# Reciprocals spread over a head's rows by DMA in fp32 instead of by products on TensorE, in a kernel of memory-augmented attention and a spectral filter

## The chip, the cores and the metric

The kernel runs on one core of a Trainium2 chip. A core has TensorE (PE, with its weight loads shown as PEld), VectorE (DVE), ScalarE (ACT), GpSimd (POOL), and SyncE (SP), which here issues nearly all DMAs. The metric is the device time of one execution in microseconds; three executions of the kernel before took 710.68, 711.77 and 715.36 us, median 711.77.

## The reference

Two independent parts share the program and are set side by side in the output. Part A is attention with a memory, 2048 tokens of 576 features, 32 heads of 18, in 4 segments of 512 tokens:

```python
for s in range(N):                                   # 4 segments
    p = _softmax(einsum("bhqd,bhkd->bhqk", qs, ks) * scale + mask)
    a_dot = einsum("bhqk,bhkd->bhqd", p, vs)
    num = einsum("bhld,bhde->bhle", phi(qs), M)
    den = einsum("bhld,bhd->bhl", phi(qs), z)[..., None] + 1e-6
    o = g * num / den + (1.0 - g) * a_dot
    M = M + einsum("bhld,bhle->bhde", phi(ks), vs)
    z = z + einsum("bhld->bhd", phi(ks))
return o.transpose(...).reshape(B, S, D) @ wo
```

M and z are zero in the first segment, so the memory counts from the second on. Part B is a two-dimensional real FFT of [2048, 576], a product with complex weights and the inverse; the change does not touch it.

## The kernel before, in words

The first half of the program (to about 356 us) does the FFT, the projections to q, k and v, and the memories M (`Mst`) and z (`zst`) of segments 1 to 3. What the change touches is the second half, `attention`, a loop over `t` from 0 to 132. **One `t` is one head step**: four segments of 32 heads make 128 steps. A step holds, for head `t+11`, the scores for the row maxima (`s1`: scores into PSUM, DVE maxima `mx` and `junk`), and for head `t` the scores again with the maximum folded in and the three exponentials on ACT (`s2`, L703, L708, L712). Every fourth step POOL zeroes the upper triangle of four heads (L716), and over the next four steps PE multiplies these heads by the values (`pv`, L731, sixteen matmuls in two batches of eight). The maxima of four heads go through POOL (`mh`, L682 and L683), a transpose on PE (L686), ACT, and a DMA that ACT issues (L692) into the row of the queries that carries them.

The unnormalised output `U` of eight heads goes to DRAM, its rows as `uD` and the softmax sums as `rD`. The normalisation follows a segment later. With 18 rows a head, the 576 rows of a segment are cut into five tiles of 126, 126, 126, 126 and 72 rows (7 heads and 4 heads), by 512 tokens; the order is `ORD = (4,0,1,2,3)`. For a segment the work is:

- `den`: z times phi(q) on PE (`pd`) to `dD`.
- `recip`, once for the softmax sums (times 1-g) and once for `den` (times g): load, add epsilon, reciprocal on DVE, gate on ACT. Before, ACT and POOL then split the result into three bf16 parts (L760 to L763), a DMA writes them to DRAM (L765), and another loads them as 96 rows of 512 (`rr`, `rd`, L769).
- `combine`: for each tile a matmul with the 0/1 table `sel` spreads the reciprocals of 7 heads over 126 rows in PSUM (`pb`, L851), DVE multiplies the tile `ux` of `uD` by it (L854 or L856), POOL adds the memory part `am` (L857, from the second combination on), ACT rounds (`oh`, L836), POOL takes the rest (`ol`, L841).
- `mem1`: for each tile a product of M with phi(q) on PE (`pn`, L804), a copy out of PSUM by ACT (L806; DVE at the end), another `pb` (L810) and a product on DVE (L811).
- `oproj`: the output projection, 16 pieces of seven matmuls for a segment (`po`, L874).

The last segment's normalisation and projection stand behind the loop (`last_tile`, `last_proj`).

The order is written by hand. Each engine runs its instructions in program order, so a wait stops all that stands behind it on that engine. Two mechanisms place the work beside the head steps: a **lane** gives one piece per step to each generator in it; the **background queue** `bg` is a list, taken in order, from which `run_bg(1.2)` takes 1.2 pieces a step. Before, `recip` is in the lane and `combine` and `mem1`, interleaved by `mixed`, in the background queue, and then `oproj`. `later(1, f)` puts an issue of a DMA at the end of the next step. All of these DMAs are in SP's queue with the loads of stacked queries and keys (`Qs`, `Ks`, L635 and L637), which are needed 3 and 8 steps later.

PSUM has one bank, `post`, for `pn`, `pb`, `pd` and `po`, and three each for the two kinds of scores. In SBUF `ux` has three buffers.

Of the kernel before, what the change touches and what calls it, by code (L numbers as in the profile page):

```python
# [363 lines left out]
def atables():  # L364
    sel=np.zeros((96,5,126),np.float32)
    for t in range(5):
        for p in range(126 if t<4 else 72):
            h=7*t+p//18
            sel[h::32,t,p]=1
# [5 lines left out]
    return dict(sel=sel.reshape(96,-1),bm=bm.reshape(126,-1),mask=mask,ident=np.eye(128,dtype=np.float32),neg1=-np.ones((2,4096),np.float32))  # L375
# [9 lines left out]
class ATT:  # L385
# [189 lines left out]
    def att_setup(s,cp):  # L575
# [10 lines left out]
        s.rrD=[d(f"rrD{i}",[96,512],BF) for i in range(4)]  # L586
        s.rdD=[None]+[d(f"rdD{i}",[96,512],BF) for i in range(1,4)]
# [20 lines left out]
    def late_setup(s,cp):  # L608

        nc,io=s.nc,s.io; q=[]  # L610
        s.sel=cp.tile([96,5,126],BF,name="sel",bufs=1); nc.gpsimd.dma_start(s.sel,io["sel"].rearrange("p (t m) -> p t m",t=5))
# [137 lines left out]
    def recip(s,src,dst,gate,eps,load,slack=0):  # L749
        nc=s.nc; tp=s.tp  # L750
        w=tp.tile([128,3,128],BF,name="rw",bufs=2); y=tp.tile([128,128],F32,name="ry",bufs=2)
# [12 lines left out]
        for _ in range(slack): yield  # L764
        nc.sync.dma_start(bass.AP(tensor=dst.tensor,offset=dst.offset,ap=[[128,128],[32*512,3],[1,128]]),w)  # L765
        yield
        yield
        r=tp.tile([96,512],BF,name=load,bufs=1)
        nc.sync.dma_start(r,dst)  # L769
        s.rc[load]=r  # L770
        yield
# [6 lines left out]
    def den(s,g,lane):  # L778
# [12 lines left out]
        def chain():  # L791
            yield
            yield
            yield
            yield from s.recip(s.dD[g],s.rdD[g],s.gt,True,"rd",2)
# [5 lines left out]
    def mem1(s,g,t):  # L801
# [4 lines left out]
        (nc.vector.tensor_copy if s.now>=119 else nc.scalar.copy)(am[:r],pn[:r])  # L806
        if g<3: s.later(1,lambda: s.pq_load(g+1,t))
        yield
# [17 lines left out]
    def combine(s,g):  # L826
# [4 lines left out]
        yield  # L831
        yield
        def high(u):
            r=126 if u<4 else 72
            s.oh[u]=tp.tile([128,512],F32R,name="oh",bufs=5); s.ol[u]=tp.tile([128,512],F32R,name="ol",bufs=5)
            (nc.vector.tensor_copy if s.now>=119 else nc.scalar.copy)(s.oh[u][:r],s.am[u][:r])  # L836
        def low(u):
            r=126 if u<4 else 72
            A,B=s.oh[u],s.ol[u]
            l=B if u<4 else tp.tile([128,512],F32R,name="ol4",bufs=1)  # L840
# [5 lines left out]
        for t in range(7+late):  # L846
            if t>1 and not late: high(ORD[t-2]); low(ORD[t-2])
            if t<5:
                i=t; t=ORD[t]; r=126 if t<4 else 72; x=xs[t]
                pb=s.post("pb")  # L850
                nc.tensor.matmul(pb[:r],s.sel[:,t,:r],s.rc["rr"],start=True,stop=True)  # L851
# [27 lines left out]
    def last_tile(s,t,rc):  # L879

        nc=s.nc; r=126 if t<4 else 72; x=s.ux[t]
        pb=s.ps.tile([128,512],F32,name="pb",tag="post")
        nc.tensor.matmul(pb[:r],s.sel[:,t,:r],s.rc[rc],start=True,stop=True)
        nc.vector.tensor_tensor(x[:r],x[:r],pb[:r],op=OP.mult)
# [27 lines left out]
    def begin(s,sm,sp,ps1):  # L912
# [3 lines left out]
        s.mg={};s.mx={};s.m2={};s.P={};s.vs={};s.rc={};s.am={};s.pq={};s.ux={};s.potag=None  # L916
# [18 lines left out]
    def homes(s):  # L935

        for n,t,b in (("oh",F32R,5),("ol",F32R,5),("am",F32,5),("pq",F32,5),("ux",F32,3),("ol4",F32R,1)): s.tp.tile([128 if n in ("oh","ol","ux","ol4") else 126,512],t,name=n,bufs=b)
# [215 lines left out]
```

## Time and profile before

| | |
|---|---|
| three executions, us | 710.68, 711.77, 715.36 |
| profiled execution, us | 710.93 |
| its span, us | 709.2 |
| PE, PEld busy | 679.2 us (96%), 501.4 us (71%) |
| DVE, ACT, POOL busy | 551.2 us (78%), 451.3 us (64%), 209.8 us (30%) |
| moved by DMA | 123.80 MB, mean 175 GB/s |
| head steps | from 356.6 us to about 668 us |

The durations are those of the profiled execution. In rows of groups the first number behind the bar is the busy time in us, the second the mean in ns of one instruction, and then comes the engine's idle time ahead of them. In rows of stretches the columns are the stretch and its length, then for PE, PEld, DVE, ACT and POOL the busy time and the count of instructions, the granted clock, the mean busy share of the sixteen DMA engines, and GB/s. Matmuls are pipelined: the durations of neighbours overlap, and what one costs is seen from the start of the next.

### The profile page before, as it was taken

Reading aid. Unit: us, or ns where it says so; the run is one execution under the profiler, and the core shown is the slowest. Engines: PE = TensorE matmul, PEld = TensorE weight load, DVE = VectorE, ACT = ScalarE, POOL = GpSimd, SP = SyncE. Lnnn points to the kernel's source line nnn. Section 1 sums busy time; section 2 is a strip of 40 time slices with the busy share of each in tenths; the row PEclk is TensorE's granted clock in tenths of the full one; section 3 lists DMA queues with packets and bytes.
Section 4 is the critical chain, followed back from the end, with each engine's and each line's share of the span. In section 5 each row is a group of like instructions: output and inputs, shape, how many; then the busy total and the mean of one; then the engine's idle time right before and its main releaser. Section 6 shows DMA issues by size and latency. Waiting matters only on the chain. (4 is left out here: it accounts for less than half of the span.)

```text
span 709.2 us, 14404 instructions
## 1 busy us (share of the span) xinstructions
PE 679.2 (96%) x4991; PEld 501.4 (71%) x4991; DVE 551.2 (78%) x1262; ACT 451.3 (64%) x986; POOL 209.8 (30%) x403
## 2 busy tenths in 40 slices
PE   4999999999999999999999899999999999999997
PEld 4988869879879879999954454445566445663487
DVE  5999979899799779787787887888657876567533
ACT  3665797485587474544378777777656776567421
POOL 5432000100200102655235333444323652235300
PEclk9999999999999999999999999999999999999999
DMA  8996455576385688899339886886656767442152
GB/s 308 289 286 171 132 159 185 162 208 203 91 234 177 167 209 294 199 253 262 110 111 207 182 175 137 197 202 159 152 131 176 190 159 158 89 127 67 28 156 82
DMA packets 71146, 123.80 MB, mean 175 GB/s; under 512 B 12184, under 2 KB 39174, under 8 KB 67482
## 3 DMA queue, kind: packets, MB, share of 16 engines
q1 hardware_dynamic: 64422, 106.89, 57.3%
q0 software_dynamic: 5632, 15.76, 8.2%
q8 instruction: 39, 0.64, 0.4%
q10 hardware_dynamic: 1020, 0.25, 0.2%
q14 instruction: 33, 0.27, 0.2%
HBM read 82.10 MB, written 39.81 MB: 172 GB/s over the span
## 5 line engine op out<-in xcount | busy, mean ns | idle before, releaser
L661 DVE CUSTOM_DVE_ANT_0 junk<-s,x 128x512 bf16<-128x512 f32 x248 | 137.0, 552 | 57.9 <-PE s L653 53.1
L716 POOL TENSOR_SCALAR_AFFINE_SELECT P<-P 128x512 f32<-128x512 f32 (+2 forms) x132 | 78.4, 625 | 113.6 <-ACT P L703 104.8
L667 DVE TENSOR_REDUCE mx<-s 128x4 f32<-128x512 f32 x128 | 87.7, 685 | 5.2 <-PE s L666 3.3
L703 ACT ACTIVATE P<-s 128x512 f32<-128x512 f32 x128 | 77.7, 607 | 12.6 <-PE s L702 4.6
L731 PE MATMUL pv<-P,vs 128*32 128x512 f32 (+3 forms) x1024 | 82.5, 439 | 0.1
L708 ACT ACTIVATE P<-s 128x512 f32<-128x512 f32 x128 | 77.5, 606 | 2.4 <-PE s L707 2.2
L712 ACT ACTIVATE P<-s 128x256 f32<-128x256 f32 x128 | 49.9, 390 | 44.7 <-PE s L711 44.2
L653 PE MATMUL s<-Ks,Qs 108*128 108x384 bf16 (+3 forms) x256 | 69.1, 301 | 1.5 <-DVE mx L667 1.2
L731 PEld LDWEIGHTS pv<-P,vs 128*32 128x32 f32 x1024 | 26.9, 109 | 45.3 <-issue 34.5
L461 PE MATMUL pj<-x,wqkh 128*128 128x512 f32 x162 | 56.5, 409 | 0.0
L653 PEld LDWEIGHTS <-Qs 108*128 108x128 bf16 x320 | 31.5, 98 | 24.4 <-issue 13.0
L205 DVE TENSOR_TENSOR Z<-t,t 128x290 f32<-128x290 f32 (+1 forms) x96 | 48.4, 555 | 0.1
L519 POOL MEMSET vt<- 128x32 f32 x16 | 2.4, 167 | 149.0 <-PE pm L529 127.7
L205 DVE TENSOR_TENSOR t<-Z 128x580 f32<-128x580 f32 x64 | 46.1, 757 | 0.0
L142 PE MATMUL f<-ftab,eh 128*128 128x290 f32 (+1 forms) x160 | 32.6, 323 | 11.8 <-DMA ftab<-ftab 9.2
L666 PE MATMUL s<-tri,idb 128*128 128x128 bf16 x256 | 43.0, 219 | 0.0
L295 PE MATMUL i<-civ,Y 128*128 128x256 f32 (+1 forms) x288 | 39.3, 289 | 0.2 <-POOL Y L280 0.2
L295 PEld LDWEIGHTS i<-civ,Y 128*128 128x128 f32 (+1 forms) x288 | 36.6, 181 | 1.0 <-POOL Y L280 0.4
L306 PE MATMUL i<-itab,T 128*128 128x290 f32 (+1 forms) x224 | 36.7, 306 | 0.0
L142 PEld LDWEIGHTS f<-ftab,eh 128*128 128x128 f32 (+1 forms) x160 | 26.1, 206 | 14.0 <-issue 8.6
L461 PE MATMUL pj<-x,wqkl 128*128 128x512 f32 x90 | 35.5, 395 | 0.0
L461 PE MATMUL pj<-xh,wqkl 128*128 128x512 f32 x90 | 35.5, 395 | 0.0
(210 smaller groups left out, 1830.2 us busy)
## 6 DMA issues: line engine op xcount, KB each, us to landing
qkD<-sp SPq DMA_DIRECT2D x32, 384.0 KB
xin<-xb SPq DMA_DIRECT2D x16, 384.0 KB
cfw<-cfw POOLq DMA_DIRECT2D x16, 384.0 KB, 4.3
civ<-civ POOLq DMA_DIRECT2D x16, 384.0 KB, 8.8
vs<-vD SPq DMA_DIRECT2D x16, 330.0 KB
vD<-vt SPq DMA_DIRECT2D x16, 311.0 KB
W<-w SPq DMA_DIRECT2D x16, 290.0 KB
yb<-yout SPq DMA_DIRECT2D x16, 290.0 KB
```

The lines of the kernel that those rows point to most:

```text
L142: nc.tensor.matmul(p[:,r,:FP],x,t,start=n==0,stop=n==6)
L205: v.tensor_tensor(o,a,b,op=op)
L295: nc.tensor.matmul(p[:m,k],Y[i][:,q,c*128:c*128+m],cc[:,hl,o:o+256],start=n==0,stop=n==5)
L461: s.nc.tensor.matmul(out,a,b,start=i==0,stop=i==len(L)-1)
L653: nc.tensor.matmul(out,Q[:108,h,128*i:128*i+128],K[:108,h,:128*(i+1)],start=True,stop=True)
L661: nc.vector.tensor_tensor_reduce(out=junk[:,:w],in0=src,in1=s.mask[:,512-w:],scale=1.0,scalar=-3.0e38, op0=OP.add,op1=OP.max,accum_out=s.m ...
L667: nc.vector.tensor_reduce(out=s.mx[k][:,hh],in_=pa.rearrange("p (b c) -> p b c",c=128),axis=mybir.AxisListType.X,op=OP.max)
L703: nc.scalar.activation(P[0][:,hh],p0,AF.Exp,scale=SC)
L708: nc.scalar.activation(P[1][:,hh],p1,AF.Exp,scale=SC)
L712: nc.scalar.activation(P[2][:,hh],p2,AF.Exp,scale=SC)
L716: nc.gpsimd.affine_select(out=x[:,r],in_=x[:,r],pattern=[[0,r.stop-r.start],[1,128]],compare_op=OP.is_ge,fill=0.0,base=0,channel_multiplie ...
L731: nc.tensor.matmul(s.pvt[32*hh:32*hh+32,128*j:],vt[:,j,19*h:19*h+32],mv[0][:,hh,mv[1]],start=j==0,stop=j>1,skip_group_check=True)
```

## The change

The reciprocals are no longer split into bf16 parts. `recip` writes 64 KB of fp32, and for each tile `bt_load` reads them back with a row repeated 18 times, so that a tile `bt` of 126 rows by 512 in SBUF holds the factors. It has three buffers, and the next load is put in SP's queue one step after a tile was used. There are 35 of these loads: 20 for the four combinations and 15 for the memory. The 35 `pb` matmuls, the table `sel`, the loads `rr` and `rd`, the ACT and POOL work of the split, and the copy out of PSUM in `mem1` go: DVE multiplies `pn` from PSUM by `bt` at once. `combine` moves from the background queue into the lane, one tile per head step; the five `mem1` become background pieces of one step each, and the background rate goes from 1.2 to 0.8. A buffer for `ol` is saved.

```diff
-    def recip(s,src,dst,gate,eps,load,slack=0):
+    def recip(s,src,dst,gate,eps):
...
         nc.scalar.activation(y,y,AF.Copy,scale=gate)
-        nc.scalar.copy(w[:,0],y)
-        nc.gpsimd.tensor_tensor(y,y,w[:,0],op=OP.subtract)
-        nc.gpsimd.tensor_copy(w[:,1],y)
-        nc.gpsimd.tensor_tensor(w[:,2],y,w[:,1],op=OP.subtract)
...
-        r=tp.tile([96,512],BF,name=load,bufs=1)
-        nc.sync.dma_start(r,dst)
...
+        nc.sync.dma_start(dst.rearrange("h (b c) -> (h b) c",b=4),y)
+    def bt_load(s):
+        if not s.bsrc: return
+        a,t=s.bsrc.pop(0); w=7 if t<4 else 4
+        x=s.tp.tile([126,512],F32,name="bt",bufs=3)
+        a=a[7*t]
+        s.nc.sync.dma_start(x[:18*w],bass.AP(tensor=a.tensor,offset=a.offset,ap=[[512,w],[0,18],[1,512]]))
+        s.bts.append(x)
...
-        (nc.vector.tensor_copy if s.now>=119 else nc.scalar.copy)(am[:r],pn[:r])
+        nc.vector.tensor_tensor(am[:r],pn[:r],s.bts.pop(0)[:r],op=OP.mult)
+        s.later(1,s.bt_load)
...
-        pb=s.post("pb")
-        nc.tensor.matmul(pb[:r],s.sel[:,t,:r],s.rc["rd"],start=True,stop=True)
-        nc.vector.tensor_tensor(am[:r],am[:r],pb[:r],op=OP.mult)
...
-    def mixed(s,g):
+    def mixed(s,g,bg):
...
-            next(c,None); yield
-            if i>=d:
-                for _ in s.mem1(g,ORD[i-d]): yield
+            next(c,None)
+            if i>=d: bg.append(s.mem1(g,ORD[i-d]))
+            yield
...
-                pb=s.post("pb")
-                nc.tensor.matmul(pb[:r],s.sel[:,t,:r],s.rc["rr"],start=True,stop=True)
+                pb=s.bts.pop(0)
+                s.later(1,s.bt_load)
...
+                    s.bsrc+=[(s.rrD[g-1],t) for t in ORD]+[(s.rdD[g],t) for t in ORD]
+                    for _ in range(3): s.bt_load()
...
-                    bg.append(s.mixed(g))
+                    yield from s.mixed(g,bg)
...
-            run_bg(1.2)
+            run_bg(0.8)
```

What moves is seen in the engines' rows. VectorE, in the first combination, steps 51 to 53 of before (each step has one `mx` and two `junk`; the product is L854):

```order
L854 TENSOR_TENSOR am<-ux,pb 72x512
L661 ISA junk,mg<-s_6324,x_2754 128x256
L661 ISA mg 128x1
L667 TENSOR_REDUCE mx<-s_6340 128x4
L661 ISA junk,mg<-s_6352,x_2754 128x512
L661 ISA mg 128x1
L854 TENSOR_TENSOR am<-ux,pb 126x512
```

and the same of the changed program (L843, L661 and L655 there), from step 49:

```order
L843 TENSOR_TENSOR am<-ux,bt 72x512
L661 TENSOR_REDUCE mx<-s_6264 128x4
L655 ISA junk,mg<-s_6273,x_2754 128x512
L655 ISA mg 128x1
L655 ISA junk,mg<-s_6281,x_2754 128x256
L655 ISA mg 128x1
L843 TENSOR_TENSOR am<-ux,bt 126x512
```

The product has moved behind the step's maxima, two steps earlier, and reads `bt` from SBUF in place of `pb` from PSUM. Further on, a product follows in each step, five in a row, where before those of `mem1` lay between them and the five took eight steps.

SyncE's queue at the same place, steps 47 to 51 of before (`rr` and `rd` are the loads that go, `Qs` and `Ks` the stacked queries and keys):

```order
L644 DMA vs<-vD_82 128x4x165
L769 DMA rd<-rdD_3340 96x512
L635 DMA Qs_3316<-qkD_72 48x4096
L769 DMA rr<-rrD_3336 96x512
L635 DMA Qs_3316<-qkD_72 32x4096
L635 DMA Qs_3316<-qkD_72 16x4096
L637 DMA Qs_3316<-reD_76 12x4096
L635 DMA Ks_3317<-qkD_72 48x4096
L825 DMA ux<-uD_3324 126x512
```

and of the changed program:

```order
L629 DMA Qs_3316<-qkD_72 48x4096
L763 DMA bt<-rrD_3336 72x1x512
L763 DMA bt<-rrD_3336 126x1x512 x2
L629 DMA Qs_3316<-qkD_72 32x4096
L629 DMA Qs_3316<-qkD_72 16x4096
L763 DMA bt<-rrD_3336 126x1x512
L815 DMA ux<-uD_3324 126x512
L631 DMA Qs_3316<-reD_76 12x4096
L763 DMA bt<-rrD_3336 126x1x512
L815 DMA ux<-uD_3324 126x512
L629 DMA Ks_3317<-qkD_72 48x4096
```

Five loads of `bt` and two of `ux` now stand among the loads of the queries; each from the fourth `bt` on waits until DVE has used an earlier tile, and what is behind it in SP's queue waits with it.

GpSimd in the second combination, steps 84 to 86 of before (L857 adds the memory part, L841 makes `ol`, L682 and L683 are `mh`):

```order
L857 TENSOR_TENSOR am<-ux,am 72x512
L682 CAST mh<-mg 128x16
L683 TENSOR_TENSOR mh<-mg,mh 128x16
L857 TENSOR_TENSOR am<-ux,am 126x512
L841 TENSOR_TENSOR ol_7830<-am,oh 72x512
L857 TENSOR_TENSOR am<-ux,am 126x512
```

and steps 81 to 85 of the changed program (L846 adds, L830 makes `ol`, L676 and L677 are `mh`, L710 zeroes the triangles):

```order
L846 TENSOR_TENSOR am<-ux,am 72x512
L846 TENSOR_TENSOR am<-ux,am 126x512
L710 AFFINE_SELECT P_7544<-P_7544 128x4x128
L710 AFFINE_SELECT P_7545<-P_7545 128x4x128 x2
L710 AFFINE_SELECT P_7546<-P_7546 128x4x128
L830 TENSOR_TENSOR ol<-am,oh 72x512
L846 TENSOR_TENSOR am<-ux,am 126x512
L676 CAST mh<-mg 128x16
L677 TENSOR_TENSOR mh<-mg,mh 128x16
L830 TENSOR_TENSOR ol<-am,oh 126x512
L846 TENSOR_TENSOR am<-ux,am 126x512
L830 TENSOR_TENSOR ol<-am,oh 126x512
```

`mh`, for which PE's transpose waits a step later, stood behind one addition; now it stands behind three additions, a subtraction and four selects.

More of the change, by code (lines that the diff above doesn't have):

```diff
@@ L585, in att_setup @@
         s.dD=[None]+[d(f"dD{i}",[32,512],F32) for i in range(1,4)]
-        s.rrD=[d(f"rrD{i}",[96,512],BF) for i in range(4)]
-        s.rdD=[None]+[d(f"rdD{i}",[96,512],BF) for i in range(1,4)]
+        s.rrD=[d(f"rrD{i}",[32,512],F32) for i in range(4)]
+        s.rdD=[None]+[d(f"rdD{i}",[32,512],F32) for i in range(1,4)]
     def stacks0(s,pool):
@@ L878, in oproj, with last_tile @@
                 yield
-    def last_tile(s,t,rc):
+    def last_tile(s,t):
         nc=s.nc; r=126 if t<4 else 72; x=s.ux[t]
-        pb=s.ps.tile([128,512],F32,name="pb",tag="post")
-        nc.tensor.matmul(pb[:r],s.sel[:,t,:r],s.rc[rc],start=True,stop=True)
-        nc.vector.tensor_tensor(x[:r],x[:r],pb[:r],op=OP.mult)
+        nc.vector.tensor_tensor(x[:r],x[:r],s.bts.pop(0)[:r],op=OP.mult)
         nc.vector.tensor_tensor(x[:r],x[:r],s.am[t][:r],op=OP.add)
@@ L1010, in attention @@
         if qu: qu.pop(0)()
-        b=s.recip(s.rD[3],s.rrD[0],s.g1,False,"rd"); next(b)
+        b=s.recip(s.rD[3],s.rrD[0],s.g1,False); next(b)
         for u in range(3): s.ux_load(3,u)
+        s.bsrc=[(s.rrD[3],0),(s.rrD[3],1),(s.rrD[3],2)]
+        for _ in range(3): s.bt_load()
+        s.bsrc=[(s.rrD[0],3),(s.rrD[0],4)]
         while qu: qu.pop(0)()
```

45 lines of the change are left out of this document (18 added, 27 removed).

## The prediction

> **What bounds the kernel now.** I read the page first, then stretches of the attention half, then single rows.
>
> ```profile
> PE 679.2 (96%) x4991; PEld 501.4 (71%) x4991; DVE 551.2 (78%) x1262; ACT 451.3 (64%) x986; POOL 209.8 (30%) x403
> ```
>
> PE is busy 96% of the span, but that is an average. The change acts only from 357 us on, and there the rows below cut the time by what runs beside the head steps. First come ten steps with nothing beside them, then the first and the second combination with its memory products, the projection between them, the third combination, and the end behind the loop.
>
> ```profile
> 406.68:426.01 19.33, 19.01 (x180) 9.82 (x178) 16.27 (x53) 15.33 (x39) 7.42 (x17) 1.00 0.85 182
> 462.07:497.90 35.83, 34.24 (x276) 16.99 (x275) 29.17 (x86) 27.05 (x63) 16.52 (x26) 1.00 0.78 180
> 553.21:589.37 36.16, 34.59 (x276) 16.80 (x275) 29.09 (x85) 26.82 (x64) 21.81 (x31) 1.00 0.74 177
> 500.64:546.56 45.92, 45.92 (x388) 30.55 (x389) 28.36 (x85) 29.00 (x70) 13.29 (x28) 1.00 0.59 140
> 639.45:666.40 26.95, 24.87 (x197) 10.50 (x199) 18.10 (x37) 19.66 (x45) 14.64 (x25) 1.00 0.19 58
> 671.40:706.00 34.60, 32.44 (x230) 30.90 (x230) 13.45 (x21) 8.10 (x19) 1.77 (x3) 1.00 0.35 107
> ```
>
> The same stretches for L703, of which each head step has one, give the steps:
>
> ```profile
> 406.68:426.01 19.33, 6.21 (x10) 1.00 0.85 182
> 462.07:497.90 35.83, 8.51 (x14) 1.00 0.78 180
> 553.21:589.37 36.16, 8.60 (x14) 1.00 0.74 177
> 500.64:546.56 45.92, 9.05 (x15) 1.00 0.59 140
> ```
>
> A bare step takes 19.33/10 = 1.93 us with PE idle for 0.03. Fifteen steps of projection take 45.92 with PE never idle: PE sets the pace, and what is taken from it there is gained. The granted clock is 1.00 throughout. But DVE has 1.63 us of work in a bare step (16.27/10), and the DMA engines are 0.85 busy: two others are close behind.
>
> ```profile
> 641.51 0.38 PE L702 MATMUL s<-Qs,Ks 110*128 110x512 bf16 x1
> 641.73 0.38 PE L851 MATMUL pb<-rr,sel 96*72 96x512 bf16 x1
> 641.94 0.38 PE L653 MATMUL s<-Ks,x 108*128 108x512 bf16 x1
> ...
> 654.04 1.12 PE L804 MATMUL pn<-pq,Mst 126*126 126x512 f32 x2
> 655.00 0.27 PE L711 MATMUL s<-x,Ks 110*128 110x256 bf16 x1
> ```
>
> From start to start a `pb` costs 0.21 us and a `pn` pair 0.96. So the first combination, 35.83 - 14 x 1.93 = 8.8 over bare steps, is 5 x 0.96 = 4.8 for `pn`, 9 x 0.21 = 1.9 for `pb` and 2.1 of stalls. The second, with ten `pb`, has 9.1 - 4.8 - 2.1 = 2.2 of stalls, and the third shows PE idle for 26.95 - 24.87 = 2.1. Old stalls: 6.4 us.
>
> **PE's part.** 35 `pb` go, 30 in the loop and 5 behind it: 35 x 0.21 = **-7.4 us**. The `pn`, `pd` and `po` stay; their places move, but each costs PE the same. ACT's copies of `pn` and the POOL work of the split were under PE's pace (ACT 27.05 of 35.83) and give nothing inside the loop.
>
> **What is late next in the combinations.** Four things compete, and only the longest counts at any moment.
>
> ```profile
> L716 POOL TENSOR_SCALAR_AFFINE_SELECT P<-P 128x512 f32<-128x512 f32 x124 | 75.0, 636 | 110.4 <-ACT P L703 101.6 <-ACT P L712 5.9 <-PE s L702 1.6
> ...
> L841 POOL TENSOR_TENSOR ol<-am,oh 126x512 fp32r<-126x512 f32 x8 | 10.2, 1275 | 15.7 <-ACT oh L836 14.8 <-PE pn L804 0.9
> ...
> L857 POOL TENSOR_TENSOR am<-ux,am 126x512 f32<-126x512 f32 x6 | 7.6, 1270 | 1.2 <-DVE ux L856 1.2
> ...
> L856 DVE TENSOR_TENSOR ux<-ux,pb 126x512 f32<-126x512 f32 x8 | 5.5, 684 | 2.6 <-PE pb L851 1.8 <-PE s L711 0.8
> ```
>
> *DVE's load.* One product in each step makes 1.63 + 0.68 = 2.3 us of DVE in a step of 1.93, five steps in a row: 1.9 us over, where before the five products took eight steps.
>
> *DVE against POOL.* The products now read both inputs from SBUF. Two rows of the FFT show what that means: the same DVE subtraction of two SBUF tiles takes 0.69 us when POOL starts after it, and 1.23 when POOL is already running.
>
> ```profile
> 21.44 0.69 DVE L131 TENSOR_TENSOR el<-eo,eh 128x512 fp32r<-128x512 f32 x1 [0.29 <-ACT eh L127]
> 21.50 1.24 POOL L132 TENSOR_TENSOR eh<-eo,eh 33x256 fp32r<-33x256 f32 x1 [1.38 <-ACT eh L127]
> ...
> 36.04 0.92 POOL L132 TENSOR_TENSOR eh<-eo,eh 33x256 fp32r<-33x256 f32 x1 [2.06 <-ACT eh L127]
> 36.28 1.23 DVE L131 TENSOR_TENSOR el<-eo,eh 128x512 fp32r<-128x512 f32 x1
> ```
>
> So each of the 15 products of the loop's combinations may take 0 to 0.54 us more; POOL is busy about half of such a stretch, so I take 0.27, 1.3 a combination. [...]
>
> *POOL.* In the second combination POOL gets five additions, five subtractions, two sets of four selects and `mh` within seven steps: 10 x 1.27 + 8 x 0.64 + 0.4 = 18.2 us in 7 x 1.93 plus two pieces of projection (1.0 each: 45.92 - 15 x 1.93 over 16 pieces and `den`) and two `pn`, 17.4. Counted from the start of step 81, the second product ends at about 2 x 1.93 + 2 x 1.0 + 0.7 = 6.6 us; then POOL has an addition, four selects, a subtraction, an addition and `mh` of step 84, 3 x 1.27 + 4 x 0.64 + 0.4 = 6.8, so `mh` is there at 13.4. PE reaches its transpose after four steps and a half, 4.5 x 1.93 + 2 x 1.0 = 10.7.
>
> ```profile
> 556.28 0.22 POOL L683 TENSOR_TENSOR mh<-mg,mh 128x16 bf16<-128x16 f32 x1
> 556.55 0.10 PEld L686 LDWEIGHTS <-mh 128*128 128x128 bf16 x1 [0.39 <-POOL mh L683]
> ```
>
> Before, PE waited 0.39 us here; after, I take 2.4 of the 2.7 (0 to 4, as other stalls give POOL time or take it). The third combination has the same heap, smaller: 1.5. The first has no additions.
>
> *The loads.* The trace has no load that repeats rows. A `bt` tile has the 252 KB of a `ux` tile, but its outermost count is 7 (or 4), not 126.
>
> ```profile
> 660.80:661.90 1.10, 1.10 (x18) 0.48 (x11) 0.00 (x0) 0.65 (x2) 0.00 (x0) 1.00 0.50 114
> ...
> 678.00:681.00 3.00, 3.00 (x24) 2.93 (x23) 0.00 (x0) 0.00 (x0) 0.00 (x0) 1.00 0.90 266
> ```
>
> In the first stretch only stores of `uD` run, with an outermost count of 18: half the DMA engines work, at 114 GB/s. In the second, mostly loads of `ux`, 0.90 of them work, at 266 GB/s. So a tile takes 252/266 = 0.95 us at one end and 252/114 = 2.2 at the other; I take the middle, 1.6, since it is a load like `ux` but with a small count like `uD`. In steps 48 to 59, 12 x 1.93 + 4 x 0.96 = 27 us, the loads that stand there already fill about 0.8 of the time (0.78 in the row), 21 us; ten tiles add 16, on the engines that they use: 37 into 27. The loads of queries and keys have three to eight steps of slack, so most of the 10 us is lateness that nobody waits for, but `bt` loads stand in the same queue. I charge 3 us for the first combination, 2 for the second (share 0.74, and two pieces of projection slow its steps) and 0 for the third (0.19); bounds 0 and 9 each for the first two. The 35 issues themselves take SP some 0.4 us each (1.28 for three in a row quoted below), under everything else. [...]
>
> *ACT's own DMA.* Late loads have a second victim:
>
> ```profile
> 397.71 6.53 DMA rD<-U
> 404.31 0.62 ACTq L692
> ```
>
> A 16 KB store behind a full queue took 6.5 us to land, and ACT, whose DMA of the maxima waits for an earlier DMA, stood still until then. In the changed program ACT's DMA of step 54 waits for the `rD` store of step 52, and that of step 86 for a `uD` store of step 85. I charge 1 us each, 0 to 3.
>
> New stalls: the first combination 3 + 1 + 2 (DVE's load and POOL against it, of 3.2, a part under the DMA waits) = 6; the second 2 + 1 + 2.4 + 1.1 = 6.5; the third 1.5 + 1.5 = 3. That is 15.5 for the old 6.4: **+9.1 us**.
>
> **The end and the start.** Behind the loop the last reciprocals become tiles by a chain:
>
> ```profile
> 676.18 1.28 SPq L825 DMA_DIRECT2D ux<-uD  x3
> 681.21 0.69 DVE L884 TENSOR_TENSOR ux<-ux,pb 126x512 f32<-126x512 f32 x1 [9.06 <-DMA ux<-uD]
> 683.53 0.40 ACT L759 ACTIVATE ry<-ry,g 128x128 f32<-128x128 f32 x1
> 686.46 0.39 SPq L765 DMA_DIRECT2D rrD<-rw  x1
> ```
>
> Three `bt` loads go behind the three `ux`, so the first product comes 1.6 us later than 681.21; from the gate (683.93) to the store, 2.5 us of ACT and POOL go. PE has projection pieces until about 686 and is idle for 34.60 - 32.44 = 2.2 us in all, of which the waits for `post` behind `pb` are half: **-1.0** (-3 to +2). At the start, the background rate of 0.8 puts two loads of the output weights beside those of phi(q), ahead of the late `rD` store above: **+0.7** (-0.5 to +2).
>
> **Sum:** -7.4 + 9.1 - 1.0 + 0.7 = +1.4 us, against the profiled execution's 710.93: **712 us**. The median of the three runs is 711.77, so this is no change that a measurement of this kernel, good to about 1%, could tell.
>
> **Rivals.** *Stalls no worse than the old ones* (faster): `bt` tiles at 0.95 us keep up, POOL's heap falls into PE's waits, and the new stalls equal the old 6.4. Then -7.4 - 1.0 + 0.3, **703 us**. For it: PE's idle time is small everywhere. Against it: shares of 0.74 to 0.85 before ten tiles are added. *The queue decides* (slower): loads of `bt` come late by the whole excess, 10 us in the first and 9 in the second combination in place of 3 and 2, since each waits in SP's queue for DVE and then lands behind queries and keys; DVE waits, and with it the maxima and PE. That gives 712 + 14 = **726 us**, 718 with half of it. It decides from the point where a tile and its share of the other loads take longer than a step with `pn`, 2.9 us. *The change does not give what it takes away*: if in the combinations DVE's 2.3 us a step set the pace, PE's 7.4 us would be slots that nobody misses, and only the stalls remain: **719 us**. Against it stands PE's idle time of 1.6 in 36 us there.
>
> **Chances.** Forecast (706 to 718) 0.45; faster rival (699 to 706) 0.18; queue (718 to 730) 0.30; lost slots (717 to 722) 0.07. The range 703 to 726 leaves out some 0.10 of the faster rival and 0.10 of the queue's; the forecast's own is 706 to 718. Faster by over 1%, below 704.7: 0.15. Slower by over 1%, above 718.9: 0.32, the queue's and a little of the lost slots. Within: 0.53.
>
> **What would show it.** PE without `pb` and DVE products of `ux` and `bt` in five steps in a row; in steps 49 to 59 DVE idle before a product "<-DMA bt", some 3 us in the first combination; a wait of PE for `mh` of 2 to 3 us in the second; products of 0.7 to 1.2 us there; the projection stretches unchanged to 0.3 us. I am wrong if DVE never waits for `bt`, or if it waits over 8 us in one combination, or if the projection stretches grow.

## The result, and the profile after

The changed kernel is **slower**: 748.42 us (median of 5 runs, 745.31 to 748.61) against 710.68 us (710.22 to 715.36) for the kernel before, a ratio of 1.0505 (95% interval 1.047 to 1.054). The forecast was 712 us with a range of 703 to 726, so the time lies far outside it, on the slow side.

The first view is the page of the changed kernel: engines' busy time, then the granted clock and the DMA engines in 40 slices.

```profile
span 746.7 us, 14332 instructions
...
PE 685.5 (92%) x4956; PEld 500.9 (67%) x4956; DVE 549.6 (74%) x1251; ACT 445.3 (60%) x970; POOL 208.5 (28%) x382
...
PEclk9999999999999999999999999897999879999999
```

PE has 35 matmuls fewer (4991 to 4956), all of them `pb`, so the change does what it says. Yet PE is busy for *longer*, 685.5 us against 679.2, although the `pb` took 7.4 us of it away: the same matmuls took 6.3 + 7.4 = 13.7 us more. This is what is left of a sum; the 7.4 is the prediction's price and was not measured by itself. The row PEclk says why PE took longer, with its 8 and 7 in two places: the granted clock fell. And PE is idle for 746.7 - 685.5 = 61.2 us, against 709.2 - 679.2 = 30.0. So the 37.5 us between the two profiled spans are

-7.4 (the `pb`) + 31.2 (idle PE) + 13.7 (PE at a lower clock) = **+37.5 us**.

Where it happens is seen in the stretches that the prediction used: ten clean steps, the first and the second combination (14 steps each, from step 48 and from step 84), the projection (15 steps), the third combination (14 steps), and the end behind the loop.

```profile
408.89:429.21 20.32, 19.18 (x180) 9.81 (x178) 16.55 (x56) 16.03 (x41) 8.77 (x18) 1.00 0.79 169
462.05:514.22 52.17, 38.91 (x273) 18.51 (x272) 29.81 (x85) 24.65 (x60) 16.05 (x26) 0.84 0.73 177
574.71:630.12 55.41, 43.34 (x304) 21.93 (x303) 31.32 (x85) 25.64 (x61) 21.95 (x32) 0.85 0.69 162
524.83:565.21 40.38, 40.38 (x347) 25.02 (x346) 27.34 (x80) 26.90 (x66) 11.00 (x22) 1.00 0.65 148
670.34:703.11 32.77, 27.84 (x216) 12.80 (x214) 18.18 (x36) 22.52 (x53) 20.70 (x25) 1.00 0.34 111
703.11:746.70 43.59, 35.18 (x276) 31.41 (x274) 14.93 (x23) 9.35 (x23) 2.17 (x7) 0.98 0.36 122
```

For the first combination and for the end, the kernel before has these rows over the same steps:

```profile
456.94:491.80 34.86, 33.27 (x273) 16.56 (x272) 28.11 (x83) 25.77 (x63) 15.21 (x27) 1.00 0.78 177
...
663.88:709.20 45.32, 39.30 (x292) 34.13 (x290) 18.02 (x28) 10.26 (x25) 5.51 (x14) 1.00 0.31 96
```

The first combination takes 52.17 us for 34.86, with PE idle for 13.26 where it was idle for 1.59, and at a clock of 0.84. In the second PE is idle for 12.07 (1.57 before), at 0.85; its 14 steps now also hold four pieces of projection, 28 matmuls, where before they held none. The projection has no idle PE, as before; its 15 steps take 40.38 us for 45.92 because at the rate of 0.8 they hold 41 matmuls, some six pieces, fewer. DMA is no busier than before in the first combination (0.73 for 0.78), although PE, DVE and ACT all wait for DMA there. The chain of waits says which transfers, here in order of time:

```profile
461.70 5.59 DMA bt<-rrD
467.31 0.69 DVE am L843
...
469.51 8.74 DMA Qs<-reD
478.30 0.34 PE s L647
478.64 0.10 PE s L660
...
485.14 0.06 PE s L660
...
489.69 6.42 DMA pq<-pqD
496.13 11.20 DMA x<-reD
```

First DVE waits for the first tile of reciprocals, and then PE waits twice for *queries* (`Qs`, and `x`, which is another stack of queries). In the timeline of PE the second of these waits, the last row ahead of it and what comes behind it read so:

```profile
504.64 0.42 PE L705 MATMUL s<-Qs,Ks 110*128 110x256 bf16 x1
507.42 0.48 PE L647 MATMUL s<-Ks,x 108*128 108x384 bf16 x1 [2.36 <-DMA x<-reD]
507.69 0.31 PE L660 MATMUL s<-tri,idb 128*128 128x128 bf16 x1
507.80 0.31 PE L647 MATMUL s<-Ks,x 108*128 108x128 bf16 x1
507.90 0.31 PE L660 MATMUL s<-tri,idb 128*128 128x128 bf16 x1
```

From start to start the L660 matmul takes 0.11 us here. In the chain above it counts 0.10 at 478.64, right behind the first wait for queries, and 0.06 at 485.14. The granted clock is 0.50 from 478.51 to 481.92 us and from 502.41 to 512.65, and 1.00 at 485.14. These waits are thus paid twice: once while PE stands (4.33 us for the first, 2.36 for the second), and once when it goes on at half the clock.

DVE's waits for `bt` are there too, and ACT's for its own DMA. (In the changed kernel L843 and L845 are the products with `bt` of the first and of the later combinations, L799 the product with `pn`, L697 an exp of each head step, L846 and L830 POOL's addition and subtraction.) First DVE in the first combination, then ACT late in the first and in the second, each from the timeline:

```profile
467.31 0.69 DVE L843 TENSOR_TENSOR am<-ux,bt 72x512 f32<-72x512 f32 x1 [1.82 <-DMA bt<-rrD]
470.04 0.69 DVE L843 TENSOR_TENSOR am<-ux,bt 126x512 f32<-126x512 f32 x1 [0.26 <-DMA bt<-rrD]
...
503.39 0.69 DVE L799 TENSOR_TENSOR am<-pn,bt 126x512 f32<-126x512 f32 x1 [5.74 <-DMA bt<-rdD]
```

```profile
500.35 0.60 ACT L697 ACTIVATE P<-s 128x512 f32<-128x512 f32 x1 [4.40 <-DMA x<-qkD]
...
606.05 0.60 ACT L697 ACTIVATE P<-s 128x512 f32<-128x512 f32 x1 [6.00 <-DMA pq<-pqD]
```

### The profile page after: what moved, and what is told of

Same layout as the page of the kernel before. It is cut to its first block, busy times and chain, and to the rows that moved or that the text cites. A ratio compares the mean times of both kernels' runs of the same rounds, so it can differ in the third digit from the quotient of the medians.

```text
span 746.7 us, 14332 instructions
## 1 busy us (share of the span) xinstructions
PE 685.5 (92%) x4956; PEld 500.9 (67%) x4956; DVE 549.6 (74%) x1251; ACT 445.3 (60%) x970; POOL 208.5 (28%) x382
## 4 chain that ended last, share of the span: by engine, by line
PE 65%; DMA 15%; DVE 7%; POOL 4%; ACT 4%; issue 3%; SPq 1%; ACTq 0%; DVEq 0%; POOLq 0%
PE pj L456 14%; PE s L647 8%; PE pjv L456 7%; PE pv L725 7%; PE po L863 5%; PE i L295 4%; PE i L306 4%; PE s L696 3%; DMA pq<-pqD 2%; DVE eo L125 2%; PE s L700 2%; POOL P L710 2%; PE pm L524 2%; DMA x<-reD 1%; PE s L660 1%
## 5 line engine op out<-in xcount | busy, mean ns | idle before, releaser
L655 DVE CUSTOM_DVE_ANT_0 junk<-s,x 128x512 bf16<-128x512 f32 x248 | 137.0, 553 | 67.7 <-PE s L647 61.3
L710 POOL TENSOR_SCALAR_AFFINE_SELECT P<-P 128x512 f32<-128x512 f32 (+2 forms) x132 | 80.7, 644 | 148.2 <-ACT P L697 138.7
L697 ACT ACTIVATE P<-s 128x512 f32<-128x512 f32 x128 | 77.5, 605 | 42.8 <-PE s L696 23.6
L661 DVE TENSOR_REDUCE mx<-s 128x4 f32<-128x512 f32 x128 | 87.7, 685 | 14.7 <-PE s L660 13.1
L725 PE MATMUL pv<-P,vs 128*32 128x512 f32 (+3 forms) x1024 | 88.8, 467 | 0.2 <-POOL P L710 0.2
L647 PE MATMUL s<-Ks,Qs 108*128 108x384 bf16 (+3 forms) x256 | 70.9, 307 | 8.7 <-DVE mx L661 5.2
L660 PE MATMUL s<-tri,idb 128*128 128x128 bf16 x256 | 44.3, 224 | 0.0
L142 PE MATMUL f<-ftab,eh 128*128 128x290 f32 (+1 forms) x160 | 32.3, 319 | 11.7 <-DMA ftab<-ftab 8.7
L647 PE MATMUL s<-Ks,x 108*128 108x384 bf16 (+3 forms) x128 | 35.1, 305 | 2.7 <-DMA x<-reD 2.4
```

Of the source, the lines that this page charges most:

```text
L647: nc.tensor.matmul(out,Q[:108,h,128*i:128*i+128],K[:108,h,:128*(i+1)],start=True,stop=True)
L655: nc.vector.tensor_tensor_reduce(out=junk[:,:w],in0=src,in1=s.mask[:,512-w:],scale=1.0,scalar=-3.0e38, op0=OP.add,op1=OP.max,accum_out=s.m ...
L660: nc.tensor.matmul(pa[:,o+w-128:o+w],s.idb,s.tri,start=False,stop=True,skip_group_check=True)
L661: nc.vector.tensor_reduce(out=s.mx[k][:,hh],in_=pa.rearrange("p (b c) -> p b c",c=128),axis=mybir.AxisListType.X,op=OP.max)
L697: nc.scalar.activation(P[0][:,hh],p0,AF.Exp,scale=SC)
L710: nc.gpsimd.affine_select(out=x[:,r],in_=x[:,r],pattern=[[0,r.stop-r.start],[1,128]],compare_op=OP.is_ge,fill=0.0,base=0,channel_multiplie ...
```

## The experiments

The theory behind the forecast was that the loads of `bt` come late but mostly beside other work. After the result there were four theories for the idle PE. A: the loads keep few DMA engines busy (where three of them run alone behind the loop, the share is 0.44, as of 7 in 16). B: their bytes are too many on any engines. C: the order, since a load waits in SP's queue for DVE and everything behind it waits too. D: not the loads at all, but DVE, POOL or the lower background rate. Times are medians; the kernel before ran beside each group, at 710.77 to 711.35 us.

### Two copies of each row: a higher DMA share

```diff
-        nc.sync.dma_start(dst.rearrange("h (b c) -> (h b) c",b=4),y)
+        for j in range(2): nc.sync.dma_start(bass.AP(tensor=dst.tensor,offset=dst.offset+512*j,ap=[[1024,32],[128,4],[1,128]]),y)
...
-        a=a[7*t]
-        s.nc.sync.dma_start(x[:18*w],bass.AP(tensor=a.tensor,offset=a.offset,ap=[[512,w],[0,18],[1,512]]))
+        a=a[14*t]
+        s.nc.sync.dma_start(x[:18*w],bass.AP(tensor=a.tensor,offset=a.offset,ap=[[512,2*w],[0,9],[1,512]]))
```

> The changed kernel, with each row of reciprocals stored twice in DRAM (one more store of 64 KB per set), so that a load of bt repeats 14 rows 9 times where it repeated 7 rows 18 times: outermost count 14 (8 for the short tile) in place of 7 (4). Same bytes, same tile, same place in the queue. Theory A (few DMA engines: the loads of bt pile up on 7 of 16 engines, and the loads of keys and queries behind them wait for these 7): the two long combinations lose most of their stalls, 715 us, 709 to 722. Theory B (bytes: 2.4 MB more per combination are too much on any engines) and theory C (order: the loads wait in SP's queue for DVE to free a buffer, and everything queued behind waits too): still 740 to 749. Under all of them DVE and POOL are as in the changed kernel.

739.45 us. Nine of the 37.6 us come back, neither A's 715 nor B's and C's 740 and over. In the first combination (462.36 to 507.49 us) the DMA share is 0.87 where the changed kernel has 0.73. A higher share went with less loss, but it is not all.

### Plain rows in place of repeated ones

```diff
-        s.nc.sync.dma_start(x[:18*w],bass.AP(...,ap=[[512,w],[0,18],[1,512]]))
+        s.nc.sync.dma_start(x[:18*w],s.uD[0][126*t:126*t+18*w])
```

> The changed kernel, with each load of bt replaced by a load of as many plain rows of uD (126, or 72, rows of 2 KB, no row read twice); the products are taken with these in place of the reciprocals, so the combined values are others, and the stored reciprocals are never read. Same bytes, place and waits, outermost count 126. Theory A: as with two copies, 714 us, 707 to 722. Theory B and theory C: 740 to 749. If reading one DRAM row 18 times is what is slow, this one is fast and the one with two copies is not: 714 against over 735.

731.82 us: between the theories again, some 17 us better. It is 7.6 below the two copies, but differs from them in three ways: 126 for 14 and 72 for 8 as the outermost counts, no second store, and no wait for the stored reciprocals. Which of these counts was not tried.

### No load of `bt`

```diff
-        x=s.tp.tile([126,512],F32,name="bt",bufs=3)
-        a=a[7*t]
-        s.nc.sync.dma_start(x[:18*w],...)
-        s.bts.append(x)
+        s.bts.append(s.woh[:126,0,:512].bitcast(F32))
```

> The changed kernel without any load of bt: each product reads a part of the output weights that lies in SBUF in the place of the reciprocals (other values), so DVE still reads two SBUF tiles, and no DMA and no buffer of bt is left. All three theories on the loads: the projected gain of 35 pb with the stalls of DVE and POOL, 703 to 710 us. Rival D (the stalls come from DVE's dense products, POOL's heap or the lower rate of the other work, not from the loads): still over 725.

710.86 us (708.36 to 715.93), the time of the kernel before: 37.6 of the 37.6 us are gone, and D falls as the main cause. But it is not the 703 that 35 missing `pb` promise. Its stretches for the three combinations, from an execution that took 715.31 us, show what is left:

```profile
461.22:496.45 35.23, 33.14 (x273) 16.88 (x272) 29.56 (x85) 24.37 (x59) 16.47 (x27) 1.00 0.81 182
556.39:596.79 40.40, 36.51 (x299) 19.66 (x300) 29.84 (x82) 25.26 (x61) 21.04 (x31) 1.00 0.78 174
636.92:674.12 37.20, 33.07 (x216) 14.11 (x214) 18.07 (x36) 22.64 (x53) 19.19 (x25) 0.82 0.17 48
```

PE is idle for 2.1, 3.9 and 4.1 us, and in the third the clock falls to 0.82. The forecast's stalls of DVE and POOL (8.5 us in the three) are thus about right in sum. With a later start (step 48 at 461.22 us for 456.94) and, in this execution, the lower clock they eat what the `pb` gave.

### The loads, read by nobody

```diff
         s.nc.sync.dma_start(x[:18*w],bass.AP(...))
-        s.bts.append(x)
+        s.bts.append(s.woh[:126,0,:512].bitcast(F32))
```

> The changed kernel with its loads of bt at their places, but nobody reads them: the products take a part of the output weights that lies in SBUF (other values, as in the kernel without these loads). So no load waits for DVE, and DVE waits for no load; what is left of the loads is their traffic and their place in SP's queue. Theory A with B (traffic: the loads of keys and queries behind them come late): 735 to 748, and PE waits for keys and queries as in the changed kernel. Theory C (the order: what costs is that DVE waits for a tile and SP's queue for DVE): 711 to 718, near the kernel without the loads.

744.19 us. Without any reader the loads still cost 33 of the 37.6 us, so DVE's waits for `bt` cost only 4: C falls as the main cause. (A load can still wait here for a transfer that lands: by the chain the one at 481.76 us was issued 0.02 us behind a landing.) The waits in the first combination, as engine, line, what it waited for, sum, times and longest:

```profile
PEld L647 <- DMA Qs<-reD: 8.7, 1, 8.7
PE s L647 <- DMA Qs<-reD: 8.4, 1, 8.4
```

One wait for queries alone has PE idle for 8.4 us. The 14 steps of the first combination, and of the second:

```profile
459.92:511.72 51.80, 37.63 (x273) 18.15 (x272) 30.13 (x85) 24.54 (x60) 16.47 (x27) 0.84 0.73 176
571.60:624.37 52.77, 41.69 (x299) 21.80 (x300) 28.27 (x82) 25.19 (x61) 20.62 (x31) 0.87 0.71 170
```

PE is idle for 14.2 and 11.1 us, 12.1 and 7.2 more than without the loads.

### The same loads from ACT's queue

```diff
-        s.nc.sync.dma_start(x[:18*w],bass.AP(...))
+        s.nc.scalar.dma_start(x[:18*w],bass.AP(...))
```

> As the kernel whose loads of bt nobody reads (other values), but these loads are issued by ACT, on its own DMA queue, so that keys and queries do not stand behind them in SP's queue. If the place in one queue is what makes keys and queries late: 711 to 720. If it is the 7 DMA engines as such, which both queues share: 730 to 748. ACT issues 35 more instructions, which may cost it up to half a microsecond each where PE waits for ACT, some 5 us in the long combinations.

753.17 us, slower still, but this run decides nothing, since ACT now stands in SP's place. Its timeline has these rows in the first combination:

```profile
470.27 0.60 ACT L697 ACTIVATE P<-s 128x512 f32<-128x512 f32 x1 [4.57 <-DMA ux<-uD]
...
490.30 0.60 ACT L697 ACTIVATE P<-s 128x512 f32<-128x512 f32 x1 [6.17 <-DMA Qs<-mts]
```

These waits are far more than the half microsecond per issue that was expected (the issues of `bt` themselves take 0.74 to 0.78 us there), and the time lies above the 730 to 748 us. Whether the place in one queue matters is left to "queries first", below.

### The same loads from plain rows, and half of them

The first of these changes the source as above. The second leaves out every second load, so that each combination has five in place of ten:

```diff
+        x=s.tp.tile([126,512],F32,name="bt",bufs=3); s.nb=getattr(s,"nb",-1)+1
...
+        if s.now>=132 or s.nb%2==0: s.nc.sync.dma_start(x[:18*w],bass.AP(...))
```

> As the kernel whose loads of bt nobody reads (other values), with each load taken from 126 (72) plain rows of uD: all ten loads, same bytes and places, outermost count 126, and no wait for the stored reciprocals. Theory A (few engines are all of it): 711 to 716, near the kernel without loads. [...]

> [...] By the prediction's account (loads that fill about 21 us of 27, and 16 us more for ten tiles) five tiles add 8 us, 29 into 27, so nearly all the lateness goes: 712 to 720. If each load costs by itself, wherever it stands, half of the loss stays: 726 to 732.

Plain rows 729.25, half of the loads 726.20. So of the 33 us that unread loads cost, about 15 go with plain rows (744.2 - 729.3) and 18 stay with the same bytes at the same places in the queue (729.3 - 710.9). The 15 are not the repeated rows' alone, since the plain rows also wait for no stored reciprocals; the two copies, which keep that wait, brought 9. Half of the loads cost half, 15 us, not the few that the prediction's account leaves of it. Their stretches over the 14 steps of the first combination, plain rows first:

```profile
462.73:509.04 46.31, 37.44 (x273) 18.09 (x272) 30.25 (x85) 24.79 (x60) 15.85 (x26) 0.89 0.91 192
```

```profile
462.58:504.91 42.33, 35.34 (x273) 17.43 (x272) 30.05 (x85) 24.51 (x60) 15.86 (x26) 0.92 0.81 178
```

PE is idle for 2.1 us without loads, 7.0 with five tiles of repeated rows, 8.9 with ten of plain rows, 14.2 with ten of repeated rows. An isolated tile of repeated rows takes 1.68 us at a DMA share of 0.44 (below), so ten are an estimated 17 us, and 12 of these turn into idle PE; five are 8 us, and 5 do. The cover is some 4 us, not the bulk. With plain rows the DMA share is 0.91, and PE still loses 6.8 us more than without loads.

### Queries first

```diff
-            if q: q.pop(0)()
+            for _ in range(4 if t%8==0 and t>=48 else 1):
+                if q: q.pop(0)()
```

> The changed kernel, with the four loads of a query stack issued at the start of each eighth step from step 48 on, ahead of the loads of bt, in place of one or two per step. Same bytes, same engines. If the short slack of the query loads decides (theory S): PE's waits for queries in steps 52, 60, 84 and 92 go, 16 us by the profile of the changed kernel, and with them most of the half clock behind them, some 10 us: 721 to 730. If the engines are full over the whole stretch, the lateness passes to the loads of bt, keys and phi(q): 740 to 750.

746.88 us, as without it. The waits of its first combination:

```profile
PE s L647 <- DVE mx L661: 8.3, 3, 6.9
...
DVE am L843 <- DMA bt<-rrD: 6.5, 1, 6.5
...
DVE am L799 <- DMA bt<-rdD: 5.6, 1, 5.6
```

No long wait for queries is left, but DVE waits for `bt` and PE for DVE, and PE's idle time there is 13.3 us, to a tenth what it was. In the second combination it falls from 12.1 to 7.2 us, but in the steps between the two it grows from 0.9 to 5.4. The lateness only changes its place. The same edit was made to the kernel before as a control, and the opposite one took slack from that kernel:

```diff
-            if q: q.pop(0)()
+            for _ in range(0 if t in (48,49,80,81) else 2 if t in (53,54,85,86) else 1):
+                if q: q.pop(0)()
```

> The kernel before with the query loads issued first in the same way, as a control: PE waits for no query there in the long combinations, so 708 to 713.

> The kernel before, with the query loads of steps 48 and 49, and of 80 and 81, issued two steps later (and the rest of that queue caught up in steps 53, 54, 85 and 86): not a byte more, only less slack. Theory S: the last load of a stack needs some 4 to 5 us and is used about three steps after its issue; two steps less leave PE waiting 2 to 5 us twice, with half clock behind it: 716 to 726. If there were three to eight steps of slack, as the prediction has it: 709 to 713.

The control took 714.60 us (709.98 to 716.92): not neutral, 4 us slower, which was not expected, so up to 4 us of a gain of "queries first" may be hidden in it. With the queries late the kernel before takes 716.57 us. The first matmul that reads the new queries, behind the first exponential of step 52, shows the slack; the kernel with late queries comes first, then the kernel before, each with the issue of the last of these loads:

```profile
464.53 0.37 SPq L637 DMA_DIRECT2D Qs<-reD  x1
...
468.90 0.48 PE L653 MATMUL s<-x,Qs 108*128 108x384 bf16 x1 [3.81 <-DMA Qs<-reD]
```

```profile
459.79 0.39 SPq L637 DMA_DIRECT2D Qs<-reD  x1
...
466.39 0.32 PE L653 MATMUL s<-x,Qs 108*128 108x384 bf16 x1 [0.77 <-DVE mg L661]
```

An issue 4.7 us later is 3.8 us too late; the matmul starts 4.4 us behind it. Already in the kernel before PE stood for 0.77 us ahead of this matmul. The row names DVE, whose result came at 466.25 us, but by the semaphores in the trace the load landed only at 466.14. So these queries landed with next to nothing to spare, not with the "three to eight steps of slack" of the prediction. (Behind step 80 no such wait shows.)

### The rate, and the mended kernels

Rate 1.2 in the changed kernel, rate 1.2 without loads of `bt`, two copies together with 1.2 up to step 47, the two causes of loss that could be taken away, and this with queries first:

```diff
-            run_bg(0.8)
+            run_bg(1.2)
...
+            run_bg(1.2 if t<48 else 0.8)
```

> The changed kernel with the other background work at a rate of 1.2 per head step again, in place of 0.8. If the loads decide: within 6 us of the changed kernel (742 to 754), since the combination runs on the lane and not at this rate; more projection work beside the steps of the next loads gives them less time per step of work left for the end. Rival D (the lower rate spreads work so that PE starves): 715 to 730.

> The changed kernel without any load of bt (products with a part of the output weights in SBUF, other values) and with the other background work at 1.2 in place of 0.8. The lower rate cost the changed kernel 5.8 us up to step 48 against the one at 1.2; if that is the loads of the output weights beside those of keys and nothing else, this kernel gets them back: 703 to 706, the faster rival of the prediction (7.4 us of pb gained, stalls as before). If the stalls of POOL and the half clock behind them decide instead: 708 to 714, as at 0.8.

> [...] If they add: 739.5 - 5.8 = 734, range 729 to 738. If the time gained at the start only moves the loads of bt into a busier stretch: 737 to 743. In both cases slower than the kernel before.

> [...] Theory S: 709 to 718, near the kernel before and near the kernel without any load of bt. If the bytes fill the stretch: 728 to 734, as without the earlier queries.

They took 743.97, 717.25, 733.08 and 734.33 us. The higher rate reaches step 48 at 456.28 us where the changed kernel does at 462.05, and two copies and the early rate add up as expected. Queries first adds nothing to these two either (734.33 for 733.08). Without loads the high rate is *worse* than the low one, 717 for 711, outside both ranges that were expected. It brings PE ahead early, but then work of the output projection is used up in the loop that would stand behind it: 12 pieces are left there in place of 15, and PE waits for the last products. This is read from the trace, and no run tests it by itself:

```profile
692.94 0.40 PE L887 MATMUL po<-woh,P 126*128 126x288 f32 x1 [2.59 <-ACT P L870]
694.97 0.74 PE L887 MATMUL po<-woh,P 126*128 126x288 f32 x2 [1.51 <-DVE P L874]
```

No version here beats the kernel before. The fastest with the change, 710.86 us, has no load at all and computes something else.

### Pauses of PE: short and long

To see what a wait costs beyond itself, pauses of the same total were put into the clean steps of the kernel before:

```diff
+    def stall(s,k):
+        nc=s.nc; pz=s.post("pz")
+        nc.tensor.matmul(pz[:,:128],s.idb,s.zz,start=True,stop=True)
+        for _ in range(k): nc.gpsimd.memset(s.zz,0.0)
+        nc.tensor.matmul(pz[:,:128],s.idb,s.zz,start=True,stop=True)
...
+            if t in (25,26,29,30,33,37,38,41): s.stall(5)     (short)
+            if t in (25,29,33,37): s.stall(11)                (long)
```

> The kernel before, with eight pauses of PE put into steps 25 to 41, where nothing but head steps runs: a small matmul reads a tile, POOL then clears that tile five times, and a second small matmul reads it, so PE waits for POOL some 1.3 us (an estimate from POOL's 0.2 us for a clear of this size); nothing of the result changes. Theory H (PE's clock halves for about 3.4 us when PE has been idle for over about 1.8 us of the 3.4 us before): no pause is long enough, clock 1.000, and the time is that of before and the pauses, 711 + 8 x 1.3 = 721, 717 to 725.

> As the kernel with eight pauses, but four of twice the length (eleven clears, some 2.6 us): the same time of waiting in all, nothing of the result changes. Theory H: most of these pauses are followed by 3.4 us at half the clock, 1.7 us each, so 3 to 7 us more than with eight short ones, 724 to 730, and the granted clock shows the windows. If a pause costs only its own length: the same time as with eight short pauses, within 2 us, and the clock stays at 1.000.

724.82 us with eight short pauses and 731.53 with four long ones. The pauses measure 1.37 to 1.43 us (11.2 in all) and 2.94 us (11.8 in all). Against 711.35, the short ones cost 13.5 and the long ones 20.2: the wait itself, and then 2 and 8 us more. Three stretches of 3.41 us around the first long pause:

```profile
409.79:413.20 3.41, 1.28 (x12) 0.88 (x12) 0.84 (x3) 0.71 (x3) 1.63 (x8) 1.00 1.04 202
413.20:416.61 3.41, 3.41 (x20) 1.71 (x22) 2.64 (x8) 2.39 (x5) 0.71 (x2) 0.50 0.49 89
416.61:420.02 3.41, 3.41 (x36) 1.71 (x24) 2.16 (x9) 2.22 (x7) 1.78 (x3) 1.00 0.01 4
```

PE idle for 2.13 of 3.41 us, then the clock at 0.50 for the next 3.41 us, then 1.00. From 406 to 460 us the mean clock is 0.81 with the long pauses, which makes 2 x 0.19 x 54 = 20.5 us at half clock and at most half of that, 10 us, of loss; 8 were measured. With the short ones it is 0.94, some 6.5 us at half clock and at most 3 us of loss; 2 were measured. Theory H holds, but for the clean 1.000 expected with short pauses, and the long ones cost 1.5 us more than its range.

## Why the prediction was wrong

*What held.* PE lost 35 `pb` and nothing else. The **price of a `bt` tile**, 1.6 us, was right: behind the loop three loads run alone, and the changed kernel's stretch there reads

```profile
719.50:722.50 3.00, 0.14 (x2) 0.00 (x0) 2.34 (x4) 0.86 (x3) 0.00 (x0) 1.00 0.44 154
```

that is 252 KB at 154 GB/s, 1.68 us, at a DMA share of 0.44. **POOL's heap**: PE's wait for `mh` was forecast at 1.5 us in the third combination and measured 1.64; in the second it was to be 2.4, is hidden behind DMA waits in the changed kernel, and measures 1.5 without the loads. **DVE against POOL**: of the 15 products in the loop that read both inputs from SBUF three took longer than 0.8 us (1.17, 1.76, 1.68 for 0.69), 2.5 us in all where 15 x 0.27 = 4 were counted; the 15 that read `pn` from PSUM all took 0.69. The second of the three, with the POOL row of the timeline and the DVE row of the chain, shows what was taken from the FFT:

```profile
585.31 1.27 POOL L830 TENSOR_TENSOR ol<-am,oh 126x512 fp32r<-126x512 f32 x1 [2.02 <-ACT oh L825]
```

```profile
585.37 1.76 DVE ux L845
```

The product started 0.06 us after POOL's subtraction and took 1.76 us.

*The step that failed* is the charge for the loads: "The loads of queries and keys have three to eight steps of slack, so most of the 10 us is lateness that nobody waits for", and from it 3 us for the first combination and 2 for the second. The excess itself, 10 and 9 us, had about the right size: PE's idle time grew by 11.7 and 10.5 us in the two, and 12 and 7 us of idle time go when the unread loads are taken away. What was wrong is that it would be waited for by nobody: in the kernel before the queries of step 52 had next to no slack. The rival "the queue decides" had the size, and it was set aside on a figure for the slack that no row carried. Its mechanism was only partly right: the loads hurt less by DVE's waits for them (4 us) or by their place ahead of the queries (no gain with queries first) than by their transfers, in a stretch that had an estimated 4 us of room for them: 18 us stay with plain rows, and 9 go with two copies, at a DMA share of 0.87 for 0.73. How much of the 18 is bytes and how much the order of the other loads stays open. The share of 0.78 misled, as a mean over 16 engines and 36 us: it stays at 0.73 while PE, DVE and ACT wait for DMA, and tiles that run alone are at 0.44. How the loads lie on the single engines was not shown.

*The term that was missing* is the clock. "The granted clock is 1.00 throughout" was read as a constant. It was 1.00 in a kernel whose PE, after 350 us, never stood for more than 1.0 us at once. With the new waits of 1.9 to 4.3 us, 41 us of the span from step 20 on are at half clock (400.0, 454.6, 468.3 and 478.5 for 3.4 us each, 502.4 and 608.2 for 10.2, 577.5 for 6.8), in which PE is idle for 9.8. Half of the other 31.2, an estimated 15.6 us, is what the clock cost by this record, near the 13.7 us that the sum leaves for longer matmuls. Rival and clock together, 726 + 13.7, are 740. What is left lies outside these two combinations, where PE is idle for 9.0 us more than before.

*Smaller misses.* **The start**: +0.7 was forecast for the rate of 0.8, and step 48 is reached 5.1 us later (462.05 for 456.94). PE's idle time up to there grew by 2.9, and two waits (2.6 and 1.86 us) were each followed by 3.4 us at half clock. **The end**: from step 127 on, 45.32 us became 43.59, but only because one piece of projection (1.0), a `pn` pair (1.0) and the `pb` went from there. PE's idle time in it grew by 2.4 us (8.4 for 6.0), where -1.0 was forecast; in the stretch of 3.00 us shown above PE is busy for 0.14. **ACT's own DMA**: 1 us each was charged; ACT stood for 4.40 and 6.00 us, of which PE was idle for 1.6 and 2.8. **The third combination**: +0.9 us of idle time was forecast, 2.8 measured (4.9 for 2.1). **DVE's waits for `bt`** are 7.8 us in the first combination, not 3.

In the prediction's own terms: its -7.4 is not contradicted (by the clock's 15.6 us PE's work fell by 9.3), and its changes in stalls, +9.1 (combinations), -1.0 and +0.7, measured +31.2 of idle time and +13.7 of clock.

## What to carry to other kernels

A DMA share below 1 was no room here: at 0.73 PE, DVE and ACT stood for transfers. Look for the share of a new load where it runs alone (0.44 for a tile), and for what runs in the very stretch, and treat its excess as lateness that PE will pay, unless a row shows the slack of each load that is pushed back. Where PE is the bound, price a wait by its length and by the half clock that follows it: here a wait of 3 us cost 5 (20.2 / 4), while two of 1.4 us cost 3.4 (13.5 / 4). And count what work that is drawn forward by a higher rate will leave uncovered later.

## What the hardware showed that was not expected

The clock windows. In the profile of the changed kernel the granted clock has 14 records between its first and its last, and each lasts 3.413 us or a multiple of that (6.827, 10.240 and so on up to 126.293). Cut on this grid from 352 us on, there are eight full-speed windows in which PE was idle for 1.85 us or more (1.85 to 3.20), and each was followed by one at 0.50. In every other full-speed window PE was idle for 1.74 us or less, and none was followed by one at 0.50. Three of the eight with what came behind them, and then two with less idle time, 1.22 and 1.74 us:

```profile
396.60:400.01 3.41, 1.11 (x12) 0.62 (x12) 1.17 (x6) 1.08 (x4) 0.41 (x2) 1.00 0.98 178
400.01:403.42 3.41, 3.41 (x24) 1.44 (x24) 1.23 (x5) 1.78 (x5) 0.00 (x0) 0.50 0.94 200
403.42:406.83 3.41, 3.41 (x34) 1.65 (x32) 2.94 (x8) 1.50 (x5) 0.00 (x0) 1.00 0.67 183
451.21:454.62 3.41, 1.55 (x13) 0.72 (x15) 3.27 (x9) 2.52 (x8) 0.16 (x2) 1.00 0.93 200
454.62:458.03 3.41, 3.41 (x25) 1.60 (x18) 1.76 (x6) 0.85 (x4) 0.27 (x2) 0.50 0.83 225
475.10:478.51 3.41, 0.21 (x2) 0.15 (x3) 1.17 (x4) 0.92 (x4) 2.04 (x4) 1.00 0.90 201
478.51:481.92 3.41, 3.41 (x20) 1.14 (x22) 1.39 (x3) 1.19 (x2) 0.00 (x0) 0.50 0.53 139
...
717.45:720.86 3.41, 2.19 (x17) 1.96 (x15) 0.70 (x2) 0.00 (x0) 0.00 (x0) 1.00 0.60 220
720.86:724.27 3.41, 1.67 (x12) 1.67 (x13) 3.38 (x6) 1.52 (x4) 0.00 (x0) 1.00 0.34 125
724.27:727.69 3.42, 3.42 (x28) 3.42 (x27) 2.64 (x5) 1.74 (x4) 0.00 (x0) 1.00 0.62 179
```

The last three rows show that the length of a wait was not all: PE stood for 2.97 us up to 722.61, but 1.22 of it lay in one window and 1.74 in the next, and the clock stayed at 1.00. A wait of 1.86 us up to 453.11 lay in one window, and 0.50 followed. Of the twelve whole windows at half clock, the seven with PE idle for at most 0.38 us were followed by full speed, the five with 0.83 to 2.83 us by another at 0.50.

The clock goes with a spread in the times of one kernel. The kernel without loads of `bt` ran between 708.4 and 715.9 us; its two executions above 715 us had the lowest mean clocks, 0.983 and 0.987, the eight others 0.990 to 0.995. In the profiled one, with a span of 713.6 us, the 37.20 us of the third combination had a mean clock of 0.82, some 13 us at half clock, with PE idle for 4.13 us in all. The pauses of 1.37 to 1.43 us also brought some half clock. So 1.85 us is a number of one profile and no limit.
